# Moving the low-word bits and the squares of the values to ScalarE in an attention-and-experts kernel

## The chip, the cores and the metric

The kernel runs on one core of one Trainium2 chip, in one launch. The metric is the device time in microseconds; the median of three runs before the change is 773.28 us (770.98 to 773.47).

## The reference

The layer is causal attention with a gated memory, followed by two feed-forward layers:

```python
local = softmax(mask(q @ k.T / 8)) @ v                  # B, H, S, D = 2, 8, 576, 64
mem_out = (phi(q) @ M_prev) / (phi(q) @ z_prev + 1e-6)  # phi(x) = elu(x) + 1
x = g * mem_out + (1 - g) * local                       # g = sigmoid(beta), per head
x = relu(x @ moe_w_in) ** 2 @ moe_w_out                 # 1152 x 512 -> 2048 -> 512
out = sum_e p[:, e] * (relu(x @ w1[e]) @ w2[e])         # 4 experts, 512 -> 1024 -> 512
```

The values are float32, except `moe_w_in` and `moe_w_out`: they come as float64, so each of their numbers is a pair of 32-bit words in memory, and the kernel makes float32 of them on the chip.

## The kernel before

The 1152 tokens are nine tiles of 128, in three chunks: two tiles, then four, then three. Attention of a chunk runs beside the first feed-forward layer of the chunk before, so that TensorE always has something to do. Four stages follow each other: an opening with the attention of the first chunk, a stage in which the first feed-forward layer runs for that chunk (matmuls `hpa` and `y`) beside the attention of the second chunk, the same for the two later chunks, and then the experts.

The first of these feed-forward stages also converts the float64 weights (function `convert`). There are 16 blocks of 128 hidden units, each with an input half and an output half, so 32 halves. For each half SP issues the load of `w64` (128 x 512 pairs of words, 512 KB, four buffers). Line 626, on ScalarE, makes `mag`, the absolute value of the high word scaled by 2^-112. Line 628, on VectorE, makes `bits`, the low word shifted right by 29, which leaves its three upper bits. Line 629, on VectorE, shifts `mag` left by 3 and ors `bits` in; line 632, on VectorE, ors the sign in. Line 635 stores the half to `w1s` for the later chunks. Then `split` (lines 81 and 82) makes two parts of it for TensorE: line 81 on ScalarE, and line 82, the rest, on GpSimd for three quarters of the halves and on VectorE for the others.

`value_scale` (line 344 on) sums the squares of all values `v`, from which a power of two for scaling them is made. It takes ten tiles of 128 x 512, four of them through the two `vstage` buffers that SP fills; line 373 squares a tile on GpSimd into one of three `sq` buffers, line 363 adds it up on TensorE in the PSUM tile `total`, and line 380 on VectorE reduces it. `total` and the first `hpa` of the feed-forward layer share one PSUM buffer, so the first `hpa` can start only when line 380 is done.

What sets the order: TensorE's order is the program's own throughout. In the opening the order of all engines is written by hand as a string of steps, in which each `z` is one step of `value_scale`. Elsewhere a scheduler with its own costs orders VectorE, ScalarE, GpSimd and SP, and it also moves some later work up into the opening. Every engine runs its own list in order; an instruction that waits holds up all that stand behind it on that engine. The same holds for SP, where a load that waits for a free buffer holds up the loads behind it.

Other names: `sc` are the scores, `atp` their transposed form after exp, `pm` the memory product (line 330), `xm` its copy on ScalarE (line 333), `phia` phi of the queries (lines 163 to 166), `xy` the transposed output of attention, `r` and `g` the activated hidden units (lines 674 to 678).

Of the kernel before, what the change touches and what calls it, by code (L numbers as in the profile page):

```python
# [12 lines left out]
F16 = mybir.dt.float16  # L13
BF16 = mybir.dt.bfloat16
I32 = mybir.dt.int32
AF = mybir.ActivationFunctionType
ALU = mybir.AluOpType
AX = mybir.AxisListType
# [33 lines left out]
def attention_then_experts(ctx, tc, qa, ka, va, qc, kc, vc, mz, beta, w1, probs, w2, out):  # L52
# [11 lines left out]
    nc = tc.nc  # L64
# [15 lines left out]
    def split(w, raw, eng):  # L80
        nc.scalar.activation(out=w[:, 0], in_=raw, func=AF.Copy)  # L81
        eng.tensor_sub(w[:, 1], raw, w[:, 0].bitcast(F32))  # L82
# [25 lines left out]
    def power(s, r, z):  # L108

        nc.vector.tensor_single_scalar(out=s.bitcast(I32), in_=s.bitcast(I32), scalar=1, op=ALU.logical_shift_right)  # L110
        for x, op, zx in ((r, ALU.bitwise_and, 127 - z), (s, ALU.bitwise_xor, z)):
            nc.vector.tensor_scalar(
                out=x.bitcast(I32), in0=s.bitcast(I32), scalar1=0x7F800000, scalar2=0x3F800000, op0=ALU.bitwise_and, op1=op
            )
            nc.vector.tensor_scalar(out=x, in0=x, scalar1=2.0**-126, scalar2=0.5, op0=ALU.max, op1=ALU.min)
            nc.vector.tensor_scalar_mul(x, x, 2.0**zx)
# [35 lines left out]
    def gates():  # L152

        nc.scalar.activation(out=bt, in_=bt, func=AF.Exp, scale=-1.0)
        yield
# [5 lines left out]
    def phi(out, e, q):  # L161

        nc.scalar.activation(out=e, in_=q, func=AF.Exp)
        yield
# [10 lines left out]
    def combine(t, pool, xl, xm, sm, guard, pv, ps, eng, nm=1, gate1=gate1):  # L175
# [16 lines left out]
        def second():  # L192
# [4 lines left out]
            cs = slice(t * P, t * P + P)  # L197
            nc.scalar.activation(out=xy[:, 0, :, cs], in_=tp, func=AF.Copy)
            return lambda: nc.vector.tensor_sub(xy[:, 1, :, cs], tp, xy[:, 0, :, cs].bitcast(F32))
# [5 lines left out]
    def opening(c0, c1, first_layer):  # L205

        sc, ph, low, gt = [c0.scores(u) for u in c0.units], c0.phis(0), [], gates()
        later = [c1.scores(u) for u in c1.units[:4]]
        xs = []
        third = (slice(0, 3), slice(3, 6), slice(6, 8))  # L210
        steps = dict(
            g=lambda: next(gt), c=lambda: next(cv), w=lambda: next(first_layer), l=lambda: c1.load(1),
            x=lambda: xs.extend(c0.combine(c0.units[i][0]) for i in (0, 2)),
            a0=lambda: xs[0][0](), a1=lambda: xs[0][1](), a2=lambda: low.append(xs[0][2]()), a3=lambda: low[0](),
            b0=lambda: xs[1][0](), b1=lambda: xs[1][1](), b2=lambda: low.append(xs[1][2]()), b3=lambda: low[1](),
        )
        sv = []
        steps["z"] = lambda: next(sv[0]) if sv else (sv.append(value_scale(aap, c1.load_v)), next(sv[0]))
        for i in range(4):
            steps[f"s{i}"] = lambda i=i: next(sc[i])  # L220
            steps[f"t{i}"] = lambda i=i: c0.turn(c0.units[i], nc.vector)
            steps[f"v{i}"] = lambda i=i: c0.values(c0.units[i])
        for i in range(4):
            steps[f"S{i}"] = lambda i=i: next(later[i])
        for i in range(2):
            steps[f"p{i}"] = lambda i=i: next(ph[i])
        for i in range(3):
            steps[f"m{i}"] = lambda i=i: c0.mem(0, third[i])
        order = (
            "s0 p0 s1 g s0 g s2 s1 s0 s1 s2 s3 p1 s2 l s3 t0 z z p0 z x t1 S0 s3 t2 m0 p1 v0 z S0 t3 m1 "  # L230
            "m2 v1 z S1 z S2 z S0 v2 a0 b0 v3 z S3 S1 a1 z S1 b1 S2 a2 b2 z S3 c S3 S2 b3 w a3 z z c"
        )
        for k in order.split():
            steps[k]()

    def attention_a(c, pool, eng, banks):
# [28 lines left out]
        def s_(u):  # L265
# [22 lines left out]
            for i in range(nh):  # L288
                cs = slice(i * kn, i * kn + kn)
                nc.scalar.activation(  # L290
                    out=a[:, cs], in_=a[:, cs], func=AF.Exp, bias=nb[:, h0 + i:h0 + i + 1], scale=0.125,
                    accum_out=sm[:, h0 + i:h0 + i + 1],
# [3 lines left out]
        def t_(u, eng=None):  # L296
# [9 lines left out]
            else:  # L306
                nc.scalar.activation(out=at[:, 0:n], in_=tp[:, 0:n], func=AF.Copy)
            at_[u] = at
# [35 lines left out]
    def value_scale(pool, load_v):  # L344

        total = ps_h.tile([P, 512], F32, tag="h", name="total")
        ones = pool.tile([P, P], BF16, tag="ones", name="ones", bufs=1)
        nc.gpsimd.memset(ones, 1.0)
        parts = [va_t[b, r].rearrange("p h d -> p (h d)") for r in range(2) for b in range(B)]
        late = []  # L350

        def stage(b, k):
            x = pool.tile([P, 4, P], F32, tag="vstage", name="vstage", bufs=2)
            nc.sync.dma_start(out=x, in_=vc[b, :, :, k].rearrange("j p d -> p j d"))
            return x.rearrange("p j d -> p (j d)")

        todo = [(b, k) for k in (3, 4) for b in range(B)]
        n = len(parts) + len(todo) + B
        squares = []

        def add():
            i, sq = squares.pop(0)
            nc.tensor.matmul(total, lhsT=ones, rhs=sq, start=(i == 0), stop=(i == n - 1))

        for i in range(n):
            if 2 <= i < 2 + len(todo):
                parts.append(stage(*todo[i - 2]))
            if i == 4 + len(todo) - 2:
                load_v(2)
                parts += [va_t[b, 2].rearrange("p h d -> p (h d)") for b in range(B)]  # L370
            x = parts[i]
            sq = pool.tile([P, 512], BF16, tag="sq", name="sq", bufs=3)
            nc.gpsimd.tensor_mul(sq, x, x)
            if squares:
                add()
            squares.append((i, sq))
            yield
        add()
        yield
        nc.vector.tensor_reduce(out=vs, in_=total, axis=AX.X, op=ALU.add)  # L380
        power(vs, vi, 77)
        nc.vector.tensor_mul(gate1v, gate1, vi[:, 0:1].to_broadcast([P, H]))
        yield
# [224 lines left out]
    def convert(pool):  # L608

        todo = [x for g in range(n1 + 2) for x in ((g, 0), (g - 2, 1)) if 0 <= x[0] < n1]  # L610
        words = {}

        def fetch(i):
            if i < len(todo):
                f, half = todo[i]
                words[i] = pool.tile([P, DM, 2], I32, tag="w64", name="w64", bufs=4)
                nc.sync.dma_start(out=words[i].rearrange("p n t -> p (n t)"), in_=w1[f, half].bitcast(I32))

        for i in range(2):
            fetch(i)  # L620
        for i, (f, half) in enumerate(todo):
            fetch(i + 2)
            w64 = words.pop(i)
            mag = pool.tile([P, DM], F32, tag="mag", name="mag")

            nc.scalar.activation(out=mag, in_=w64[:, :, 1].bitcast(F32), func=AF.Abs, scale=2.0**-112)  # L626
            bits = pool.tile([P, DM], I32, tag="bits", name="bits", bufs=8)
            nc.vector.tensor_single_scalar(out=bits, in_=w64[:, :, 0], scalar=29, op=ALU.logical_shift_right)  # L628
            nc.vector.scalar_tensor_tensor(  # L629
                out=bits, in0=mag.bitcast(I32), scalar=3, in1=bits, op0=ALU.logical_shift_left, op1=ALU.bitwise_or  # L630
            )
            nc.vector.scalar_tensor_tensor(
                out=bits, in0=w64[:, :, 1], scalar=-(2**31), in1=bits, op0=ALU.bitwise_and, op1=ALU.bitwise_or
            )
            nc.sync.dma_start(out=w1s[f, half], in_=bits.bitcast(F32))
            made[f, half] = bits.bitcast(F32)
            yield
# [457 lines left out]
```

## Time and profile before

| | |
|---|---|
| median of three runs | 773.28 us |
| profiled execution, its own time | 768.09 us |
| its span | 766.3 us |
| busy: TensorE matmul | 706.8 us (92%) |
| busy: VectorE | 596.7 us (78%) |
| busy: ScalarE | 428.2 us (56%) |
| busy: GpSimd | 307.8 us (40%) |

The shares are means over stages with different limits. The experts fill the second half, where TensorE has almost no gaps. The conversion lies between 33 and 146 us, and in most of that stretch VectorE is busy all the time. In the page's slices of the span the TensorE clock is at its upper level, apart from the stretches behind a gap in TensorE's work.

### The profile page before, as it was taken

The page shows a single profiled execution, that of the slowest core. Times are in us where ns is not written, and L with a number is a line of the kernel's source. Part 1 is how long each engine was busy: PE and PEld are TensorE (multiplying, and loading weights), DVE is VectorE, ACT ScalarE, POOL GpSimd, SP SyncE. Part 2 cuts the span into 40 slices and gives each one's busy share as a digit, 9 for nine tenths or more (in the row PEclk, how much of TensorE's full clock was granted, in tenths as well). Part 3 has the DMA queues.
Part 4 walks back from the last instruction along what each step waited for, and adds up shares of the span by engine and source line. Part 5 has one row for each costly group of instructions (what it writes and reads, how often), then busy time and mean ns, then how long its engine had stood idle before and what let it go on. Part 6 is the DMA issues. An engine that isn't in the chain of part 4 may idle for free.

```text
span 766.3 us, 12975 instructions
## 1 busy us (share of the span) xinstructions
PE 706.8 (92%) x4740; PEld 511.8 (67%) x4740; DVE 596.7 (78%) x1114; ACT 428.2 (56%) x836; POOL 307.8 (40%) x303
## 2 busy tenths in 40 slices
PE   7679989897899999889989988989999999999997
PEld 5568878775677777888956555656665555555553
DVE  5869999769998875575786679999877777776763
ACT  4547666667656544786666565755544535344340
POOL 4445446444524147555532325443333132332300
PEclk9869899999999999999989999999999999999999
DMA  7666667266886563585421313323433223100002
GB/s 220 227 241 211 231 215 253 100 211 229 194 189 154 121 134 90 180 285 182 138 84 56 110 56 110 111 75 96 129 127 124 83 84 106 61 1 1 1 2 68
DMA packets 65425, 101.29 MB, mean 132 GB/s; under 512 B 32656, under 2 KB 34704, under 8 KB 65360
## 3 DMA queue, kind: packets, MB, share of 16 engines
q1 hardware_dynamic: 65216, 100.45, 42.9%
q8 instruction: 37, 0.61, 0.3%
q14 instruction: 28, 0.23, 0.1%
q10 hardware_dynamic: 144, 0.00, 0.0%
HBM read 82.87 MB, written 10.75 MB: 122 GB/s over the span
## 4 chain that ended last, share of the span: by engine, by line
PE 52%; DVE 25%; issue 7%; ACT 7%; POOL 4%; DMA 3%; SPq 1%; DVEq 0%; POOLq 0%; ACTq 0%
PE o L987 18%; PE pe L893 16%; PE y L685 6%; POOL w L82 2%; DVE a L171 2%; PE hpb L88 2%; DVE wu L857 2%; PE hpc L88 2%; PE hpa L88 2%; DVE bits L629 2%; PE pv L554 2%; DVE bits L628 1%; DMA raw<-in_w 1%; PE sc L277 1%; DVE h L914 1%
## 5 line engine op out<-in xcount | busy, mean ns | idle before, releaser
L987 PE MATMUL o<-w,g 128*128 128x512 f16 x864 | 220.2, 382 | 6.5 <-ACT junk L694 2.2
L893 PE MATMUL pe<-xs,wu 128*128 128x256 f16 (+1 forms) x1344 | 200.5, 289 | 5.8 <-DVE h L914 5.7
L893 PEld LDWEIGHTS <-wu 128*128 128x128 f16 x1344 | 132.6, 99 | 76.6 <-issue 9.8
L987 PEld LDWEIGHTS <-g 128*128 128x128 f16 x864 | 84.7, 99 | 77.0 <-issue 4.1
L685 PE MATMUL y<-g,w 128*128 128x256 f32 (+2 forms) x576 | 124.8, 350 | 1.3 <-POOL w L82 0.7
L82 POOL TENSOR_TENSOR w<-wraw,w 128x512 fp32r<-128x512 f32 x49 | 71.5, 1461 | 105.8 <-ACT w L81 98.0
L908 ACT ACTIVATE g<-h 128x512 f16<-128x512 f32 (+1 forms) x64 | 43.4, 678 | 109.2 <-DVE h L914 109.1
L685 PEld LDWEIGHTS y<-g,w 128*128 128x128 f32 x576 | 94.4, 191 | 11.8 <-POOL w L82 0.9
L923 POOL TENSOR_TENSOR u<-u,p 128x256 f32<-128x256 f32 (+1 forms) x32 | 30.3, 948 | 125.3 <-ACT p L922 114.9
L860 POOL TENSOR_TENSOR ws<-raw 128x256 f32<-128x256 f32 x32 | 24.7, 772 | 118.4 <-issue 97.8
L909 DVE SCALAR_TENSOR_TENSOR g<-h,g 128x512 f16<-128x512 f32 (+1 forms) x64 | 50.9, 796 | 22.1 <-ACT g L908 21.9
L914 DVE SCALAR_TENSOR_TENSOR h<-pe,u 128x256 f32<-128x256 f32 (+1 forms) x96 | 43.1, 452 | 24.3 <-PE pe L893 17.2
L88 PE MATMUL hpb<-xy,w 128*128 128x512 f32 x192 | 52.9, 411 | 7.1 <-DVE r L675 5.5
L857 DVE SCALAR_TENSOR_TENSOR wu<-ws,wpow,wu 128x512 f16<-128x512 f32 x64 | 50.5, 828 | 3.6 <-ACT wu L868 3.6
L793 DVE SCALAR_TENSOR_TENSOR w<-raw,wpow,w 128x512 f16<-128x512 f32 x64 | 48.2, 755 | 0.7 <-ACT w L792 0.6
L171 DVE CUSTOM_DVE_ANT_0 a<-sc,mask 128x384 f32<-128x384 f32 (+4 forms) x80 | 36.3, 476 | 15.7 <-PE sc L277 9.7
L82 POOL TENSOR_TENSOR w<-bits,w 128x512 fp32r<-128x512 f32 x24 | 37.7, 1570 | 26.2 <-ACT w L81 23.7
L88 PE MATMUL hpa<-xy,w 128*128 128x256 f32 x192 | 37.6, 323 | 10.9 <-ACT mag L626 7.1
L88 PEld LDWEIGHTS hpb<-xy,w 128*128 128x128 f32 x192 | 35.7, 194 | 16.8 <-DVE r L675 8.0
L792 ACT ACTIVATE w<-raw,wpow 128x512 f16<-128x512 f32 x64 | 45.1, 709 | 0.1
L81 ACT ACTIVATE w<-wraw 128x512 fp32r<-128x512 f32 x64 | 39.5, 623 | 9.9 <-PE y L685 7.4
L88 PE MATMUL hpc<-xy,w 128*128 128x384 f32 x192 | 39.3, 350 | 6.1 <-POOL w L82 2.5
(160 smaller groups left out, 1270.8 us busy)
## 6 DMA issues: line engine op xcount, KB each, us to landing
raw<-in_w SPq DMA_DIRECT2D x64, 512.0 KB, 3.4
w<-in_w SPq DMA_DIRECT2D x32, 512.0 KB, 4.3
wraw<-w1s SPq DMA_DIRECT2D x64, 256.0 KB, 3.0
w1s<-bits SPq DMA_DIRECT2D x32, 256.0 KB, 2.2
kraw<-in_kc SPq DMA_DIRECT2D x8, 576.0 KB, 4.2
vraw<-in_vc SPq DMA_DIRECT2D x8, 320.0 KB, 3.4
qraw<-in_qc SPq DMA_DIRECT2D x4, 512.0 KB, 4.1
out<-acc SPq DMA_DIRECT2D x8, 256.0 KB, 2.1
```

Of the source, the lines that this page charges most:

```text
L82: eng.tensor_sub(w[:, 1], raw, w[:, 0].bitcast(F32))
L88: nc.tensor.matmul(acc, lhsT=w[:, a, kk * P:(kk + 1) * P], rhs=xy[:, b, kk, t0:t0 + n], start=(i == 0), stop=(i == 3 * NK - 1),)
L171: nc.vector.tensor_tensor_reduce(out=dst, in0=sc, in1=msk, op0=ALU.add, op1=ALU.max, scale=1.0, scalar=-3.0e38, accum_out=m)
L685: nc.tensor.matmul(yacc[d], lhsT=w[:, a, d * P:(d + 1) * P], rhs=g[:, b], start=(f == 0 and i == 0 and d % per == 0), stop=(f == n1 - 1 an ...
L792: nc.scalar.activation(out=w0, in_=x, func=AF.Copy, scale=s)
L793: nc.vector.scalar_tensor_tensor(out=w1, in0=x, scalar=s, in1=w0, op0=ALU.mult, op1=ALU.subtract)
L857: nc.vector.scalar_tensor_tensor(out=w[:, 1, ks], in0=x, scalar=s1, in1=w[:, 0, ks], op0=ALU.mult, op1=ALU.subtract)
L893: nc.tensor.matmul(acc, lhsT=w[:, wa, k, kk * P:kk * P + P], rhs=x[:, xb, kk], start=(m == 0), stop=(m == 5))
L908: nc.scalar.activation(out=g[:, 0], in_=hm, func=AF.Relu)
L909: nc.vector.scalar_tensor_tensor(out=g[:, 1], in0=hm, scalar=0.0, in1=g[:, 0], op0=ALU.max, op1=ALU.subtract)
L914: nc.vector.scalar_tensor_tensor(out=out, in0=acc, scalar=HID, in1=x, op0=ALU.mult, op1=ALU.add)
L987: nc.tensor.matmul(outs[t], lhsT=g[:, gb, r:r + P], rhs=w[:, wa], start=(p == 0 and m == 1 and k == 0), stop=(p == 3 and m == 0 and k == 2),)
```

## The change

Two instructions move to ScalarE. Line 628 (line 630 after) becomes an activation with the function Copy: it reads byte 3 of the low word, which is its top byte, as an 8-bit integer at a stride of eight bytes, multiplies it by 1/32, subtracts 31/64 and writes the result as a 32-bit integer, which gives the same three bits. Line 373 (line 374 after) becomes an activation with the function Square. Buffers, loads and all matmuls stay.

```diff
-            nc.gpsimd.tensor_mul(sq, x, x)
+            nc.scalar.activation(out=sq, in_=x, func=AF.Square)
...
-            nc.vector.tensor_single_scalar(out=bits, in_=w64[:, :, 0], scalar=29, op=ALU.logical_shift_right)
+            nc.scalar.activation(out=bits, in_=w64.bitcast(U8)[:, :, 3], func=AF.Copy, scale=2.0**-5, bias=-31.0 / 64)
```

TensorE's list is the same instruction for instruction. On the other engines the scheduler's order changes up to the end of the conversion. Three places matter. (Line numbers after are one or two higher.)

ScalarE in the opening, from the exponentials of the second score tile on, before:

```order
L163 ACTIVATE phia<-qa 128x512
L290 ACTIVATE a,sm<-a,nb 128x128 x8
L333 ACTIVATE xm<-pm 128x3x2x65
L163 ACTIVATE phia<-qa 128x512
L333 ACTIVATE xm<-pm 128x3x2x65
L333 ACTIVATE xm<-pm 128x2x2x65
L290 ACTIVATE a,sm<-a,nb 128x256 x4
L198 ACTIVATE xy<-tp 128x4x128 x2
L626 ACTIVATE mag<-w_444 128x512
```

And from the same place after:

```order
L291 ACTIVATE a,sm<-a,nb 128x128 x4
L374 ACTIVATE sq<-va_0_153 128x512
L374 ACTIVATE sq<-va_0_155 128x512
L374 ACTIVATE sq<-va_1_232 128x512
L291 ACTIVATE a,sm<-a,nb 128x128 x4
L164 ACTIVATE phia<-qa 128x512
L334 ACTIVATE xm<-pm 128x3x2x65
L374 ACTIVATE sq<-va_1_234 128x512
L334 ACTIVATE xm<-pm 128x3x2x65
L334 ACTIVATE xm<-pm 128x2x2x65
L374 ACTIVATE sq<-vstage 128x512 x2
L164 ACTIVATE phia<-qa 128x512 x2
```

The squares now stand between the exponentials and behind the copies of `pm`; the squares of `vstage` come after the last of these copies.

SP in the opening, from the first two loads of `vstage` on, before:

```order
L354 DMA vstage<-in_vc 128x4x128 x2
L736 DMA mzt<-in_mz 64x1040
L354 DMA vstage<-in_vc 128x4x128
L250 DMA ka_705<-in_ka 128x512 x2
L354 DMA vstage<-in_vc 128x4x128
L259 DMA va_2_364<-in_va 128x512
L259 DMA va_2_366<-in_va 128x512
L617 DMA w_444<-in_w 128x1024
```

And after:

```order
L355 DMA vstage<-in_vc 128x4x128 x2
L738 DMA mzt<-in_mz 64x1040
L251 DMA ka_705<-in_ka 128x512 x2
L252 DMA qa<-in_qa 128x512 x2
L355 DMA vstage<-in_vc 128x4x128 x2
L260 DMA va_2_364<-in_va 128x512
L260 DMA va_2_366<-in_va 128x512
L618 DMA w_444<-in_w 128x1024
```

The later two loads of `vstage` stay ahead of the last values and of the first weights `w_444`; the loads of `ka` and `qa` moved up before them.

VectorE in the middle of the conversion, before (line 171 is the masked maximum over scores, line 286 its scaled negative for the exponential, line 675 the square of the hidden units):

```order
L632 SCALAR_TENSOR_TENSOR bits<-w_830,bits 128x512
L171 ISA a,mx<-sc,mask 128x384
L171 ISA mx 128x1
L675 SCALAR_TENSOR_TENSOR r<-hpa,r 128x256
L286 TENSOR_SCALAR nb<-mx 128x1
L628 TENSOR_SCALAR bits<-w_917 128x512
L82 TENSOR_TENSOR w_1034<-bits,w_1034 128x512
L629 SCALAR_TENSOR_TENSOR bits<-mag,bits 128x512
L171 ISA a,mx<-sc,mask 128x384
```

And after:

```order
L634 SCALAR_TENSOR_TENSOR bits<-w_830,bits 128x512
L677 SCALAR_TENSOR_TENSOR r<-hpa,r 128x256
L172 ISA a,mx<-sc,mask 128x384
L172 ISA mx 128x1
L287 TENSOR_SCALAR nb<-mx 128x1
L631 SCALAR_TENSOR_TENSOR bits<-mag,bits 128x512
L634 SCALAR_TENSOR_TENSOR bits<-w_917,bits 128x512
L83 TENSOR_TENSOR w_1034<-bits,w_1034 128x512
```

The shift is gone from VectorE's list; the two instructions that or the parts together now both come after ScalarE's two.

## Rows read from the trace of the kernel before

**Rows 1.** windows, busy us of each engine (instructions), granted clock, DMA
```profile
core 0: us, PE busy (x) PEld busy (x) DVE busy (x) ACT busy (x) POOL busy (x), PEclk, DMA share, GB/s
33.00:40.00 7.00, 0.09 (x1) 0.00 (x0) 6.76 (x16) 6.54 (x17) 1.81 (x2) 0.75 0.42 147
60.00:143.00 83.00, 75.05 (x681) 66.02 (x680) 81.23 (x164) 56.43 (x134) 43.73 (x34) 0.96 0.67 226
143.00:160.50 17.50, 17.04 (x167) 15.45 (x168) 10.46 (x27) 10.28 (x24) 7.08 (x7) 1.00 0.20 66
```

**Rows 2.** the chain that ended last, shares by line, in 100 to 120 us
```profile
by line: issue 24.7%; DVE bits L629 22.0%; DVE bits L628 18.6%; DVE a L171 12.0%; DVE bits L632 10.0%; DVE w L82 6.0%; DVE nb L286 3.2%; DVE xy L199 3.0%; ACT w L81 2.7%; ACT a L290 1.1%; DVE mx L171 0.5%; DVE r L675 0.4%; DVEq L628 0.2%; A
```

**Rows 3.** VectorE groups by form, 60 to 143 us: busy us, mean ns, idle
```profile
L628 DVE TENSOR_SCALAR bits<-w 128x512 int32<-128x512 int32 x24 | 20.2, 856 | 0.0
...
L629 DVE SCALAR_TENSOR_TENSOR bits<-mag,bits 128x512 int32<-128x512 int32 x24 | 20.5, 861 | 0.0
```

**Rows 4.** timeline of VectorE: start us, length us, instruction
```profile
118.18 0.41 DVE L628 TENSOR_SCALAR bits<-w 128x512 int32<-128x512 int32 x1
...
123.55 1.55 DVE L628 TENSOR_SCALAR bits<-w 128x512 int32<-128x512 int32 x1
```

**Rows 5.** timeline of GpSimd, the same place
```profile
123.53 1.28 POOL L82 TENSOR_TENSOR w<-bits,w 128x512 fp32r<-128x512 f32 x1
```

**Rows 6.** groups by form in 60 to 143 us, ScalarE
```profile
L626 ACT ACTIVATE mag<-w 128x512 f32<-128x512 f32 x24 | 15.9, 668 | 1.7 <-DMA w<-in_w 1.5 <-ACT at L307 0.2
```

**Rows 7.** timeline of ScalarE: two L626 one behind the other
```profile
131.85 1.26 ACT L626 ACTIVATE mag<-w 128x512 f32<-128x512 f32 x2
```

**Rows 8.** groups by form, whole run, ScalarE at 1024 elements
```profile
L868 ACT ACTIVATE wu<-ws,wpow 128x1024 f16<-128x1024 f32 x32 | 36.4, 1139 | 3.3 <-POOL ws L865 3.3
```

**Rows 9.** timeline of TensorE in the opening
```profile
13.60 1.06 PE L363 MATMUL total<-sq,ones 128*128 128x512 bf16 x2
14.46 1.09 PE L302 MATMUL atp<-ident,a 128*128 128x128 f32 x4
15.48 1.39 PE L277 MATMUL sc<-ka,qa 64*128 64x128 f32 x8
17.11 0.63 PE L302 MATMUL atp<-ident,a 128*128 128x128 f32 x4 [0.24 <-ACT a L290]
19.17 1.47 PE L330 MATMUL pm<-mzd,phia 128*128 128x130 f32 x6 [1.43 <-DVE phia L166]
...
22.86 1.28 PE L330 MATMUL pm<-mzd,phia 128*128 128x130 f32 x10
...
40.20 2.90 PE L88 MATMUL hpa<-xy,w 128*128 128x256 f32 x12 [7.11 <-ACT mag L626]
```

**Rows 10.** timeline of GpSimd in the opening
```profile
9.26 2.04 POOL L373 TENSOR_TENSOR sq<-va 128x512 bf16<-128x512 f32 x2 [4.91 <-DMA va<-in_va]
...
17.53 1.04 POOL L373 TENSOR_TENSOR sq<-vstage 128x512 bf16<-128x512 f32 x1 [0.19 <-PE atp L302]
```

**Rows 11.** timeline of ScalarE in the opening
```profile
16.98 0.39 ACT L290 ACTIVATE a<-a,nb 128x128 f32<-128x128 f32 x1
...
33.07 0.66 ACT L626 ACTIVATE mag<-w 128x512 f32<-128x512 f32 x1
```

**Rows 12.** timeline of the DMA queue (SP) in the opening: issues
```profile
18.60 0.38 SPq L354 DMA_DIRECT2D vstage<-in_vc  x1
...
24.85 1.39 SPq L617 DMA_DIRECT2D w<-in_w  x3
```

**Rows 13.** DMA issues in 0 to 60 us: count, KB each, us to landing
```profile
vstage<-in_vc SPq DMA_DIRECT2D x4, 256.0 KB, 4.7
```

**Rows 14.** the chain that ended last, in order of time, 38 to 53 us
```profile
39.45 0.60 DVE vs L380
...
46.75 4.37 POOL w L82
...
51.16 0.58 PE hpa L88
```

More of the change, by code (lines that the diff above doesn't have):

```diff
@@ L15 @@
 I32 = mybir.dt.int32
+U8 = mybir.dt.uint8
 AF = mybir.ActivationFunctionType
```

## The prediction

> **What bounds the kernel now.** I read the table of windows first, then the chain that ended last in the stretch that the change touches, then the groups and the order of time there, and at last the opening.
>
> The conversion divides the first 160 us into three. In 60 to 143 us VectorE is busy 81.2 of 83 us, TensorE 75.1, ScalarE 56.4, GpSimd 43.7 [rows 1]. TensorE's figure there is not its need: it passes 681 matmuls in 83 us, while behind the conversion, in 143 to 160.5, the same mixture goes through at 167 in 17.5 us with TensorE busy 17.04 of them [rows 1]. At that pace 681 take 681 x 0.105 = 71.4 us. So TensorE has some 11 us to spare, and VectorE, with 98% busy, is what the stretch lasts. The chain agrees: in 100 to 120 us it runs through VectorE, with L628 at 18.6% and L629 at 22.0% [rows 2]. From 143 on TensorE is the bound, and stays it for most of the rest; I expect nothing there but a shift.
>
> Before 60 us it is another matter: in 33 to 40 TensorE does next to nothing [rows 1], and its first `hpa` at 40.20 [rows 9] follows the end of the reduction of `total` at 39.45 + 0.60 on VectorE [rows 14], whose PSUM buffer it takes. (The row names a ScalarE instruction as releaser, but the `total` buffer fits to 0.15 us.)
>
> **The stretch of the conversion.** Removed there: 24 of the 32 shifts, 20.2 us of VectorE at a mean of 856 ns [rows 3]. One takes 0.41 us by itself, but 1.55 when it starts just behind a GpSimd instruction: the one at 123.55 lasts to 125.10, and GpSimd's, begun at 123.53, to 124.81 [rows 4, 5]. So of the 20.2 us about 24 x 0.41 = 9.8 are work and 10.4 are waiting for GpSimd. The work goes for certain. The waiting goes only if no other VectorE instruction meets the same GpSimd instruction in its place. L629 also lies at 861 ns [rows 3]. Bounds for what VectorE needs after: 81.2 - 20.2 = 61.0 us, and 81.2 - 9.8 = 71.4 us.
>
> The Trainium skill, "SBUF — State Buffer", section "Who interferes with whom", says that VectorE and GpSimd share one pair of ports, which an instruction holds to its end, and that VectorE wants it in its two-port modes and also for any two inputs from SBUF. The trace agrees as far as the pair at 123.5 us shows. By that rule L629 and L632, with two SBUF inputs each, inherit most of the waiting, and the upper bound is the better one; it would lengthen the stretch to no more than TensorE needs anyway.
>
> Added: 24 byte conversions on ScalarE. No row shows an 8-bit input. The nearest row is L626, which reads the same tile at the same stride of 8 bytes: 668 ns [rows 6], and two behind each other take 1.26 us, so 0.6 us each in a queue [rows 7]. As lower end I take 0.5, a little below the nearest row, since fewer bytes are read; as upper end 1.1, what an activation with twice the elements takes (1139 ns) [rows 8], for the case that small elements at a stride go at half the rate. I take 0.6, the nearest row. ScalarE's need becomes 56.4 + 24 x 0.6 = 70.8 us (68 to 83).
>
> So after the change three engines need about the same in this stretch: TensorE 71.4, ScalarE 70.8, VectorE 61 to 71. None can be beaten, so the floor is 71.4 and the most to be had 11.6 us. It will not come to the floor: VectorE reached 98% as the only full engine, but now VectorE's L629 waits for ScalarE, ScalarE's exponentials wait for VectorE's maxima, and both lists are in fixed order, so a wait of one passes to the other. I take 77 us (93% of the fullest): **-6 us**, ends 0 and -11.6.
>
> **The opening.** Removed: ten squares from GpSimd. Added: ten on ScalarE, at 0.6 us like the bytes. On GpSimd the first two ran at 9.26 for 2.04 us [rows 10], long before TensorE summed them at 13.60 [rows 9]. On ScalarE they stand behind the exponentials of the third score tile, so they start at 16.98, where now those of the fourth start [rows 11]. TensorE's list is unchanged: the two sums stand ahead of the transposes of 14.46, the scores and the transposes of 17.11. The second sum can start at 16.98 + 1.2 = 18.2 and ends at about 18.7; then 1.09 + 1.39 + 0.63 = 3.1 us of TensorE work follow, and the first `pm` starts at 21.8 instead of 19.17: 2.6 us late [rows 9]. It waited for VectorE's `phia` till 19.17, which the idle GpSimd would have let come earlier; that gain is covered by the sums.
>
> The second loss follows on SP. The first square of `vstage` ran at 17.53 [rows 10] and released the third `vstage` load at 18.60 [rows 12]. After, it stands behind the copies of all `pm`, whose last matmuls began at 22.86 and ran 1.28 [rows 9]: with the 2.6 late they end at 26.8, the copy at 27.3, and the square at 27.9. So the third load is issued at 27.9, 9.3 late; behind it in the queue are the fourth, the last values and the weights, whose issue goes from 24.85 [rows 12] to about 30. A `vstage` load lands 4.7 us after issue [rows 13], so the third arrives at 32.6. In ScalarE's list four squares, four exponentials and the two `xy` copies are still to follow before the first `mag`, ten at 0.6 us or a little less: 5.5 us. It goes from 33.07 [rows 11] to about 38, and with it the two halves, the reduction of `total` and the first `hpa`: 40.20 becomes about 45, **5 us late**.
>
> Part of this comes back at once. The third weight was late before: GpSimd's L82 began at 46.75 and took 4.37 us, and the third block's `hpa` had to wait for it to 51.16 [rows 14], 11.0 us behind the first. The two `phia` exponentials that stood between the conversions have moved up, and VectorE's part of `phia` with them, so GpSimd has less to fight with there and L82 can take the 1.28 us of rows 5, 3.1 less: 45 + 11.0 - 3.1 = 52.9 against 51.16. I take **+1.7 us** at 52.9 us; ends -1 (the loads land early) and +5 (nothing comes back).
>
> **Sum.** -6 + 1.7 = -4.3 us on the profiled execution's 768.09, of which the span is 766.3; that is 763.8. The median of the runs before is 773.28, higher by a factor 1.0068, and the same factor gives 769.0. I predict 769.0 us. A difference under 0.3% (2.3 us) can't be told from no change here.
>
> **The rivals.**
> - The waiting moves on. L629 and L632 take over the shift's waits, VectorE needs 71.4, ScalarE 70.8, and the waits between them cost more than I take: the stretch lasts 80, -3 + 1.7 gives 772.0. For it: L629 already lies 0.2 us above its unhindered time. Against it: GpSimd has as much time as before and fewer takers.
> - ScalarE becomes the bound at once. If the byte form takes 1.1 us, ScalarE needs 83 us, the stretch is what it was, and +1.7 remains: 775.0. Against it: an activation on 32-bit input at the same stride shows no such cost.
> - Slower: the opening isn't won back. It is the chain square, `vstage` load, weights: if the third load comes at 28 and the conversion starts with no lead, ScalarE has both to catch up and to serve the layer, so that every block's weights come just late; the stretch gains 1 us, the opening costs 5: +4, 777.3. It decides when the first `hpa` starts after 46 and the stretch still takes over 80. For it: ScalarE's need, 85% of the old stretch, leaves little to catch up with. Against it: the gap before 51.16 [rows 14] falls away whatever the lead.
> - TensorE at its floor: the stretch takes 72, -11 + 1.7: 763.9. For it: the scheduler has put exponentials and maxima early. Against it: three full engines in step.
> - That the change is none can be left out: the lists show the instructions moved.
>
> **Chances.** Forecast (765 to 771) 0.49, TensorE's floor 0.10, waiting moves on 0.13, ScalarE the bound 0.08, opening lost 0.20. Faster by over 0.3%: the first two less a small part of the forecast, 0.57. Within: the next two, 0.22. Slower: 0.21. The range takes in the floor's half and the slow case: 761 to 778; the forecast's own range is 765 to 771.5.
>
> **What the profile after would show.** The first `total` at 17.5 to 18 and the first `pm` near 21.8; the third `vstage` load issued near 28; the first `mag` near 38 and the first `hpa` near 45; the third block at 52 without the stall. The byte conversions at 0.65 us and 0.6 in a queue. In the stretch VectorE below 95%, ScalarE above 88%, L629 and L632 with a mean at or above 0.86, and the chain going through ScalarE and TensorE rather than VectorE alone. The first layer would end at about 156 instead of 160.5, and everything behind it keep its length. The prediction is wrong if the stretch keeps 83 us or falls under 73, or if `hpa` begins by 42 or only after 48.

## The result, and the profile after

The change makes the kernel faster, in one series by about what the forecast said and in the other by about twice as much. Median 759.69 us against 772.13 us of the kernel before in the same rounds (a quotient of 0.984); the ratio on record is 0.987, 95% interval 0.9824 to 0.9916. A second series (last experiment) gave 763.13 against 767.34, ratio 0.994, 0.9918 to 0.9962. By these ratios the gain is 0.6 to 1.3%, and the two intervals do not overlap, so series of one program differ by more than an interval says. 769.0 was forecast, 0.55% below the median that it started from (773.28), with a range of 761 to 778: 759.69 lies 1.3 us below that range, 763.13 in it. The profiled execution took 762.13 us (span 760.1), 6.0 less than the one before. (Line numbers after are one or two higher.)

Where the time went is read best from four marks in TensorE's order, which is the same in all these kernels: the starts of the first `hpa`, the first `hpb` (the first layer is over), the first `hpc`, and TensorE's last run of matmuls.

| start, us | first hpa | first hpb | first hpc | last run |
|---|---|---|---|---|
| before | 40.20 | 160.30 | 310.19 | 754.06 |
| after | 45.65 | 151.94 | 302.45 | 747.81 |
| difference | +5.45 | -8.36 | -7.74 | -6.25 |

So the opening lost 5.45 us, the first layer won 13.8, and 2.1 us were lost behind it, where the change touches nothing. (Each kernel's trace is one execution, and the first `hpa` varies from one to the next, as the last experiment shows.)

The windows of the kernel after come first, columns as in [rows 1]; the second ends where as many matmuls have passed as in 60 to 143 before:

```profile
33.00:40.00 7.00, 3.45 (x22) 2.19 (x20) 5.83 (x18) 6.73 (x20) 0.00 (x0) 1.00 0.71 276
...
60.00:133.50 73.50, 71.43 (x680) 63.20 (x679) 67.86 (x140) 65.00 (x153) 42.20 (x34) 1.00 0.74 249
...
134.00:152.00 18.00, 17.02 (x169) 15.31 (x168) 14.49 (x27) 12.60 (x30) 8.13 (x8) 1.00 0.26 83
```

The 680 matmuls that took 83 us [rows 1] now take 73.5. TensorE is busy 97% of that, VectorE 92%, ScalarE 88%. Of the 9.5 us, 5.9 are gaps of TensorE (7.95 before, 2.07 now) and 3.6 are its busy time (75.05 before, 71.43 now), the granted clock being 0.96 before and 1.00 now. The first 60 us end nearly level: 301 matmuls begun before, 298 after.

VectorE's and ScalarE's groups after, in 60 to 130 us, columns as in [rows 3]; the first fence is VectorE, the second ScalarE:

```profile
L634 DVE SCALAR_TENSOR_TENSOR bits<-w,bits 128x512 int32<-128x512 int32 x21 | 23.4, 1116 | 0.3
L631 DVE SCALAR_TENSOR_TENSOR bits<-mag,bits 128x512 int32<-128x512 int32 x20 | 20.5, 1026 | 3.8 <-ACT bits L630 3.6
```

```profile
L630 ACT ACTIVATE bits<-w 128x512 int32<-128x512 uint8 x21 | 14.1, 672 | 0.0
L627 ACT ACTIVATE mag<-w 128x512 f32<-128x512 f32 x21 | 14.1, 670 | 0.0
```

The byte conversion costs what the neighbour on 32-bit numbers costs. On VectorE the shift is gone, but the two instructions behind it have grown from 0.85 to 1.03 and 1.12 us: a half needed 0.81 + 0.85 + 0.86 = 2.52 us of VectorE before (means of the same window) and needs 2.14 after. Saved are 0.38 us, the shift's work without its waits. So the waits for GpSimd were handed on, as the Trainium skill's "SBUF — State Buffer", section "Who interferes with whom", lets expect of instructions with two inputs in SBUF.

The chain of waits after, shares by line, in 60 to 100 us and in 100 to 120 us:

```profile
by line: DVE bits L634 27.5%; issue 20.1%; DVE bits L631 17.2%; DVE a L172 10.9%; DVE r L677 4.6%; ACT bits L630 3.1%; DVE xl L190 3.0%; ACT mag L627 2.4%; DVE nb L287 2.3%; DVE w L83 1.7%; DVE xy L200 1.7%; ACT a L291 1.5%; ACT w L82 1.3%;
...
by line: PE sc L278 25.9%; PE y L687 25.3%; PE hpa L89 21.7%; PE pv L322 12.5%; PE atp L303 10.8%; DVE bits L634 2.6%; issue 2.2%; DVE mx L172 0.4%; DVE a L172 0.2%; DVEq L631 0.1%
```

VectorE still sets the first part; from 100 us on TensorE does, where before it was VectorE [rows 2].

The opening after, in order of time, first TensorE (the rows that answer to [rows 9]), then SP's issues (to [rows 12]):

```profile
18.27 1.10 PE L364 MATMUL total<-sq,ones 128*128 128x512 bf16 x2 [3.96 <-ACT sq L374]
...
20.16 2.07 PE L278 MATMUL sc<-ka,qa 64*128 64x128 f32 x8
22.17 1.12 PE L303 MATMUL atp<-ident,a 128*128 128x128 f32 x4
23.08 1.51 PE L331 MATMUL pm<-mzd,phia 128*128 128x130 f32 x6
...
45.65 2.90 PE L89 MATMUL hpa<-xy,w 128*128 128x256 f32 x12 [7.50 <-ACT mag L627]
...
53.25 0.62 PE L89 MATMUL hpa<-xy,w 128*128 128x256 f32 x3
```

```profile
29.17 0.93 SPq L355 DMA_DIRECT2D vstage<-in_vc  x2
...
31.16 1.38 SPq L618 DMA_DIRECT2D w<-in_w  x3
```

This is the forecast chain: late sums, late `pm`, late squares of `vstage`, late loads, late weights. What it cost came back before 60 us, because in the kernel before something else went wrong there. GpSimd before, at [rows 14]'s 46.75 (two L82 in one row), then VectorE before at the same place, and the windows before:

```profile
46.75 5.61 POOL L82 TENSOR_TENSOR w<-bits,w 128x512 fp32r<-128x512 f32 x2 [5.86 <-ACT w L81]
```

```profile
46.80 0.76 DVE L628 TENSOR_SCALAR bits<-w 128x512 int32<-128x512 int32 x2
47.47 1.29 DVE L629 SCALAR_TENSOR_TENSOR bits<-mag,bits 128x512 int32<-128x512 int32 x2
48.67 1.29 DVE L632 SCALAR_TENSOR_TENSOR bits<-w,bits 128x512 int32<-128x512 int32 x2
```

```profile
52.00:60.00 8.00, 8.00 (x57) 7.46 (x57) 3.53 (x10) 4.16 (x10) 3.03 (x4) 0.69 0.30 114
```

Six VectorE instructions ran back to back from 46.80 to 49.96, each at its unhindered time, and GpSimd's L82 did not get through until they were done. TensorE waited for it, and behind that gap its granted clock was 0.69 from 52 to 60. After, the same eight microseconds ran at full clock:

```profile
52.00:60.00 8.00, 7.61 (x81) 6.75 (x79) 7.93 (x11) 7.11 (x15) 4.09 (x4) 1.00 0.77 268
```

Behind the first layer 1.6 of the 2.1 us have a visible place, the first block of `hpc`, first before, then after:

```profile
310.91 3.22 PE L88 MATMUL hpc<-xy,w 128*128 128x384 f32 x17 [0.28 <-DVE xy L199]
```

```profile
303.18 4.78 PE L89 MATMUL hpc<-xy,w 128*128 128x384 f32 x17 [0.29 <-DVE xy L200]
```

The same 17 matmuls at two levels of the clock; in 302.45 to 308 the granted clock is 0.69. Of the 14 profiled executions of this study, 6 show 3.2 us here and 8 show 4.8, and the run with the byte conversion alone showed each once. So these 1.6 us belong to the execution and not to the change.

### The profile page after: what moved, and what is told of

It reads as the page before. It is cut to its first block, busy times and chain, and to the rows that moved or that the text cites. A ratio compares the mean times of both kernels' runs of the same rounds, so it can differ in the third digit from the quotient of the medians.

```text
span 760.1 us, 12986 instructions
## 1 busy us (share of the span) xinstructions
PE 706.0 (93%) x4740; PEld 511.6 (67%) x4740; DVE 584.4 (77%) x1082; ACT 448.6 (59%) x878; POOL 293.6 (39%) x293
## 4 chain that ended last, share of the span: by engine, by line
PE 55%; DVE 21%; ACT 9%; issue 7%; POOL 3%; DMA 3%; SPq 1%; DVEq 0%; POOLq 0%; ACTq 0%
PE o L989 18%; PE pe L895 16%; PE y L687 6%; PE hpb L89 3%; PE hpc L89 3%; DVE wu L859 2%; DVE bits L634 2%; PE pv L555 2%; DVE bits L631 2%; DVE a L172 2%; POOL w L83 1%; PE hpa L89 1%; PE sc L487 1%; PE sc L278 1%; DMA raw<-in_w 1%
## 5 line engine op out<-in xcount | busy, mean ns | idle before, releaser
L83 POOL TENSOR_TENSOR w<-wraw,w 128x512 fp32r<-128x512 f32 x49 | 72.2, 1475 | 107.2 <-ACT w L82 106.1
L89 PE MATMUL hpc<-xy,w 128*128 128x384 f32 x192 | 40.9, 361 | 6.1 <-POOL w L83 2.5
L82 ACT ACTIVATE w<-wraw 128x512 fp32r<-128x512 f32 x64 | 39.6, 624 | 11.0 <-PE y L687 8.8
L83 POOL TENSOR_TENSOR w<-bits,w 128x512 fp32r<-128x512 f32 x24 | 35.4, 1480 | 25.4 <-ACT w L82 25.4
L89 PE MATMUL hpa<-xy,w 128*128 128x256 f32 x192 | 35.7, 313 | 7.5 <-ACT mag L627 7.5
```

Of the source, the lines that this page charges most:

```text
L89: nc.tensor.matmul(acc, lhsT=w[:, a, kk * P:(kk + 1) * P], rhs=xy[:, b, kk, t0:t0 + n], start=(i == 0), stop=(i == 3 * NK - 1),)
```

## The experiments

My theory after the result: the layer won because VectorE's work went down to what TensorE needs, the waits only moved, and the squares on ScalarE gain nothing. (The or instructions below are the two that put the parts of a weight together, L629 and L632 before, L631 and L634 after.) The rivals: the squares do their share, or VectorE's waits for GpSimd still hold the layer, or ScalarE does.

### Each half of the change alone

`e1_bits_only`, the kernel after with the squares back on GpSimd:

```diff
-            nc.scalar.activation(out=sq, in_=x, func=AF.Square)
+            nc.gpsimd.tensor_mul(sq, x, x)
```

> The bits go to ScalarE, the squares stay on GpSimd. If the opening's delay is a loss that the first blocks only cover up, the first hpa starts at 39 to 41 us instead of 45.7, the layer from there to the first hpb lasts 107 to 110 us (120.1 before, 106.3 after), and the time is 3 to 5 us below the changed kernel. Rival: the third block's weights set the pace and the delay costs nothing, then the first hpa starts early but the first hpb comes at 152 all the same, and the time is that of the changed kernel within 2 us.

Measured: 757.06 us, ratio 0.981 (0.9765 to 0.9856). First `hpa` at 42.90, first `hpb` at 149.80: a layer of 106.9 us, as after the whole change (106.3), begun 2.75 us earlier. The byte conversion alone gives the gain of the layer. The first `hpa` came later than the 39 to 41 expected, and the time doesn't tell the two kernels apart: 2.6 us by the medians, with intervals that overlap, and each is 0.984 of the median before in its own rounds.

`e2_squares_only`, the kernel before with the squares on ScalarE (the same line the other way round).

> The squares go to ScalarE, the shift stays on VectorE. If the squares only delay the opening, the first hpa starts at 45 to 46 us, the layer lasts 115 to 120 us, and the time is 0 to 4 us above the kernel before. Rival: taking the squares off the port that GpSimd and VectorE share makes the opening faster, then the time is 1 to 3 us below before.

Measured: 765.66 us, ratio 0.994 (0.9913 to 0.9967): faster, so my expectation failed. The rival had the sign but not the reason, since the opening isn't faster: the first `hpa` starts at 42.25, 2 us late (I had expected 5 to 6), but the first `hpb` at 156.63, 3.7 us early. GpSimd, then VectorE, shows why, at the place of the stall:

```profile
47.20 1.36 POOL L82 TENSOR_TENSOR w<-bits,w 128x512 fp32r<-128x512 f32 x1 [4.28 <-ACT w L81]
...
49.40 1.75 POOL L82 TENSOR_TENSOR w<-bits,w 128x512 fp32r<-128x512 f32 x1
```

```profile
46.98 1.86 DVE L628 TENSOR_SCALAR bits<-w 128x512 int32<-128x512 int32 x2
```

L82 took 1.36 us. Here VectorE's two shifts, begun at 46.98, took 1.86 us instead of 0.76: one of them waited for GpSimd, not GpSimd for six of VectorE's. In 52 to 60 TensorE then had the full clock and 68 matmuls instead of 57:

```profile
52.00:60.00 8.00, 7.38 (x68) 6.63 (x67) 7.90 (x15) 4.83 (x11) 3.64 (x3) 1.00 0.81 266
```

So in these traces the squares won by moving the opening, so that one unlucky meeting came out the other way; the byte conversion breaks that meeting too, since the shifts are gone.

The layer comes apart at its fourth block. A block has 12 `hpa`; counted are the us from the first `hpa` to the 37th, and from there to the last, the 192nd, all by their starts:

| | first three blocks | fourth block to last `hpa` |
|---|---|---|
| before | 19.97 | 94.99 |
| e2_squares_only | 14.00 | 95.24 |
| e1_bits_only | 15.40 | 85.33 |
| after | 14.87 | 85.27 |

The squares alone win in the first three blocks, where the stall was, and nothing behind them; the byte conversion wins 9.7 us behind them, and spares the stall as well. (In a second execution of the last two kernels, `e11_bits_only_again` and `e12_change_again`, it was 15.40 and 15.38, 85.34 and 85.31.)

`e8_early_squares` is the kernel after with the first two `z` steps of the hand-written order, and the load step `l`, moved up to right behind the first tiles' exponentials:

```diff
-"s0 p0 s1 g s0 g s2 s1 s0 s1 s2 s3 p1 s2 l s3 t0 z z p0 z x ...
+"s0 p0 s1 g s0 g s2 l s1 s0 z z s1 s2 s3 p1 s2 s3 t0 p0 z x ...
```

> The changed kernel with the first two squares written earlier in the opening, behind the first tile's exponentials, where ScalarE waits for a load. TensorE's first two sums then come at 13 to 15 us instead of 18.3, the first pm at 19 to 22 instead of 23.1, the first hpa at 43 to 45 instead of 45.6. If the delay of the opening counts, the time falls by 1 to 2 us; if the first blocks take it up anyway (as the equal counts at 60 us say), it stays within 1 us of the changed kernel.

Measured: 757.36 us, ratio 0.9864 (0.9816 to 0.9912), which can't be told from the change's 0.987. The first `hpa` started at 42.75 instead of 45.65 and the first `hpb` at 149.08 instead of 151.94, so in its trace the 2.9 us were kept up to there; at the first `hpc` (301.88) only 0.6 of them are left, and the time of the rounds doesn't resolve it.

### How full are the engines

`e4_byte_twice`, the kernel after with the byte conversion done a second time into a tile that nothing reads:

```diff
+            twice = pool.tile([P, DM], I32, tag="twice", name="twice")
+            nc.scalar.activation(out=twice, in_=w64.bitcast(U8)[:, :, 3], func=AF.Copy, scale=2.0**-5, bias=-31.0 / 64)
```

> The changed kernel with each byte conversion done twice, the second into a tile that nobody reads: 32 x 0.55 to 0.6 us more on ScalarE, 14 us of it in the stretch. If ScalarE still has room there (its need 71 of 72 us says no), the layer lasts under 109 us; if ScalarE is as full as its sum says, the layer grows from 106.3 by 8 to 14 us and the time by as much.

Measured: 772.78 us, ratio 1.0029 (0.9989 to 1.0069), by the ratios 0.9 to 1.6% or 7 to 12 us over the changed kernel (its two series), and all of the gain gone. 32 conversions of 0.55 us in a queue are 17.6 us of ScalarE, of which 7 to 12 came out in the time. So I estimate that ScalarE had some 5 to 11 us to spare. The one trace (of an execution of 778.39 us) has the loss in the layer, which lasts 125.8 us:

```profile
60.00:130.00 70.00, 65.74 (x539) 58.45 (x540) 49.86 (x112) 59.89 (x137) 30.12 (x25) 0.84 0.60 199
```

But TensorE's granted clock was 0.84 there (1.00 after the change), and ScalarE was busy 59.89 us of 70, no more than after the change (61.91). How much of the loss is ScalarE's queue and how much the clock, this trace doesn't show, and no size is taken from it but the conversion's own, 0.67 us.

`e3_no_shift` is the kernel before with the shift taken from VectorE and given to nobody; the three low bits are missing from the weights (`zero` is a tile that is filled with zeros once, at the start):

```diff
-            nc.vector.tensor_single_scalar(out=bits, in_=w64[:, :, 0], scalar=29, op=ALU.logical_shift_right)
...
-                out=bits, in0=mag.bitcast(I32), scalar=3, in1=bits, op0=ALU.logical_shift_left, op1=ALU.bitwise_or
+                out=bits, in0=mag.bitcast(I32), scalar=3, in1=zero, op0=ALU.logical_shift_left, op1=ALU.bitwise_or
```

> The kernel before with the shift left out altogether: the instruction that ors the three bits in reads a constant tile of zeros in their place, so the low bits are missing in the weights; nothing is added to ScalarE. If VectorE's own work was what the shift cost and ScalarE has room for the bytes, the layer lasts 106 to 110 us as with the bits on ScalarE, and L629 and L632 rise from 0.86 us to 0.95 or more, since they inherit the waits for GpSimd. If ScalarE is the bound after the change, this one's layer is shorter than that by 3 us or more. If the waits vanish with the shift, L629 stays at 0.86 or below.

Measured: 757.54 us, ratio 0.9824 (0.9769 to 0.9879), no better than with the conversion on ScalarE. The two or instructions took 0.84 and 1.15 us (I had expected 0.95 or more of both), 0.28 us more than before in sum, so some of the shift's waits are among them. Its layer took 110.2 us, longer than the 106.3 after the change, and from the fourth block on 90.1 against 85.3; in 60 to 90 us its chain of waits holds 15.4% for loads of the weights, which the change's chain doesn't show. Had ScalarE been the bound after the change, this layer should have come out 3 us shorter or more; it is 3.9 longer, but the late loads hide what it would have been without them. Why the loads come late there I didn't follow up.

### What VectorE's waits are still worth

`e5_gpsimd_fills` leaves GpSimd its place in the first layer but makes its instruction one that only writes; the second parts of the weights are zero there:

```diff
-        eng.tensor_sub(w[:, 1], raw, w[:, 0].bitcast(F32))
+        if c == 0 and eng is nc.gpsimd:
+            nc.gpsimd.memset(w[:, 1].bitcast(F32), 0.0)
+        else:
+            eng.tensor_sub(w[:, 1], raw, w[:, 0].bitcast(F32))
```

`e6_no_sign` is the kernel after without the instruction that ors in the sign (L634; the signs of the weights are missing). `e7_before_gpsimd_fills` is the kernel before with the diff of `e5_gpsimd_fills`.

> The changed kernel, but in the first layer GpSimd fills its share of the weights' low parts with zeros instead of subtracting, so that it reads nothing there (the low parts of these weights are missing in the result). If VectorE's inherited waits for GpSimd bound the stretch after the change, L631 and L634 fall from 1.03 and 1.12 us to 0.7, VectorE's busy share in 60 to 130 us falls from 93% below 80%, and the layer from the first hpa to the first hpb shortens from 106.3 to under 103 us. If TensorE bounds it, the waits vanish just the same, but the layer keeps 105 to 107 us.

> The changed kernel without the instruction that ors the sign into the weights (the signs are missing): 32 x 0.6 us less on VectorE, ScalarE and GpSimd as they were. If VectorE bounds the stretch, the layer shortens from 106.3 by 3 to 8 us; if TensorE or ScalarE does, it stays within 2 us.

> The kernel before, with GpSimd filling zeros instead of subtracting as in the run above (low parts missing). It leaves the shift on VectorE and takes the waits away. If the shift cost the layer only its own 0.4 us each, the layer stays above 112 us (120.1 before). If the waits for GpSimd were as large a part, L628, L629 and L632 fall to 0.42, 0.69 and 0.69 us and the layer comes to 105 to 110 us, as far as moving the shift took it.

| | us | ratio (95%) | first hpa to first hpb | fourth block to last hpa |
|---|---|---|---|---|
| before | | | 120.1 | 94.99 |
| after | 759.69 | 0.987 (0.9824 to 0.9916) | 106.3 | 85.27 |
| e5_gpsimd_fills | 757.24 | 0.9848 (0.9803 to 0.9893) | 103.5 | 82.72 |
| e6_no_sign | 756.41 | 0.9841 (0.9804 to 0.9878) | 104.9 | 82.88 |
| e7_before_gpsimd_fills | 748.47 | 0.9744 (0.9698 to 0.979) | 101.6 | 82.89 |

The windows in 60 to 130 us carry the reading, first of the kernel after and of `e6_no_sign`, then, with VectorE's groups, of `e5_gpsimd_fills` (lines are three higher there) and of `e7_before_gpsimd_fills` (L631 is its shift):

```profile
60.00:130.00 70.00, 68.31 (x651) 60.60 (x650) 64.59 (x131) 61.91 (x145) 39.65 (x32) 1.00 0.75 249
60.00:130.00 70.00, 69.92 (x671) 62.04 (x670) 44.91 (x116) 64.12 (x150) 39.00 (x33) 1.00 0.79 259
```

```profile
60.00:130.00 70.00, 70.00 (x665) 62.41 (x665) 56.05 (x140) 64.58 (x153) 26.43 (x33) 1.00 0.78 260
...
L637 DVE SCALAR_TENSOR_TENSOR bits<-w,bits 128x512 int32<-128x512 int32 x22 | 18.8, 854 | 0.3
L634 DVE SCALAR_TENSOR_TENSOR bits<-mag,bits 128x512 int32<-128x512 int32 x22 | 16.0, 726 | 1.9 <-ACT bits L633 1.7
```

```profile
60.00:130.00 70.00, 69.86 (x671) 61.83 (x669) 64.40 (x156) 53.10 (x128) 23.16 (x31) 1.00 0.71 239
...
L632 DVE SCALAR_TENSOR_TENSOR bits<-mag,bits 128x512 int32<-128x512 int32 x22 | 15.7, 720 | 0.0
L635 DVE SCALAR_TENSOR_TENSOR bits<-w,bits 128x512 int32<-128x512 int32 x22 | 15.5, 714 | 0.0
L631 DVE TENSOR_SCALAR bits<-w 128x512 int32<-128x512 int32 x21 | 13.4, 650 | 0.3 <-DMA w<-in_w 0.3
```

With the waits or with an instruction taken from VectorE in the changed kernel, TensorE is busy 70.00 and 69.92 of 70 us, and the layer gets only 1.4 to 2.8 us shorter: after the change VectorE's waits cost 3 us at most. (The layer of `e5_gpsimd_fills` falls between the two cases that I had set, that of `e6_no_sign` in the case of TensorE or ScalarE as the bound.) In the kernel before they cost more: with the shift still on VectorE and most of the waits taken away, TensorE is full as well, and the layer is shorter than the 105 to 110 expected. From the fourth block on the three take the same 82.7 to 82.9 us, which I read as TensorE's floor; the change comes within 2.6 us of it, and `e7_before_gpsimd_fills` has the shorter layer because its first three blocks take 13.6 us and not 15.6 or 16.4. What bounded the layer before was the two engines getting in each other's way as much as the shift's own work: without most of the waits it is at the floor with the shift in place.

### Taking GpSimd out of the way without leaving work out

That points to a version to run: line 83 of the first layer all on VectorE. It adds work to VectorE but leaves GpSimd little to meet it with. The four were timed together on one chip, with the changed kernel and the byte conversion alone beside them:

```diff
-            on_vector = ((f % 4 == 3, f % 4 == 3), (f < 3, f % 4 == 3), (False, f % 2))[c][half]
+            on_vector = ((True, True), (f < 3, f % 4 == 3), (False, f % 2))[c][half]
```

> The changed kernel, but in the first feed-forward layer line 83 runs on VectorE for all halves instead of for a quarter of them, so that GpSimd no longer meets VectorE there except for g, xl and xm. If what is left of VectorE's waits is worth the 3 us that the runs with GpSimd memsets showed: L631 from 1026 and L634 from 1116 ns to about 0.72 us (41 x 0.35 = 14 us off in 60 to 130), 16 more L83 at 0.68 (11 us on), VectorE's busy time falls by some 3 us, TensorE is busy 69.5 or more of 70 us, the layer takes 103 to 105 us from first hpa to first hpb (106.3 after the change), and the time is 754 to 757, ratio 0.979 to 0.983. Rival: L83 waits for ScalarE's line 82 and in VectorE's list holds up the shift and the maxima behind it, so that the layer takes 107 or more, ratio 0.987 or above.

> The byte conversion on ScalarE, the squares on GpSimd as before the change, and line 83 of the first layer all on VectorE. If the squares on ScalarE are worth nothing beside the byte conversion, it is as fast as the run with the squares on ScalarE beside it, or up to 4 us faster because the first hpa starts at 42 to 43 instead of 45.6: 751 to 757, ratio 0.974 to 0.983. Rival: the squares on ScalarE win 0.6% here too, as they did alone, and this one is 3 to 5 us slower than the run beside it.

> The run with the byte conversion alone again, beside the changed kernel on one chip, to settle whether the squares take away part of its gain. If both edits fill the same ScalarE, the squares cost 1 to 4 us here: ratio 0.980 to 0.984 against 0.984 to 0.988 of the whole change. If the 0.6% that the squares won alone adds to it, this one is the slower of the two by 3 to 5 us.

> The changed kernel as it is, in the same series of rounds: ratio 0.984 to 0.988 by its first measurement (0.987, 0.9824 to 0.9916). If the byte conversion alone is better by 1 to 4 us it shows in this pair; if the squares add 0.6%, this one is 3 to 5 us faster than it.

| | squares on | line 83 on | us | ratio (95%) | first hpa | first hpb | first hpc | last run |
|---|---|---|---|---|---|---|---|---|
| e12_change_again | ScalarE | 3/4 GpSimd | 763.13 | 0.994 (0.9918 to 0.9962) | 44.61 | 151.46 | 304.46 | 749.35 |
| e11_bits_only_again | GpSimd | 3/4 GpSimd | 756.23 | 0.9847 (0.9826 to 0.9869) | 39.56 | 146.44 | 297.32 | 740.80 |
| e9_rest_on_vector | ScalarE | VectorE | 753.65 | 0.982 (0.9796 to 0.9844) | 43.06 | 146.02 | 295.95 | 741.45 |
| e10_bits_only_rest_on_vector | GpSimd | VectorE | 750.96 | 0.979 (0.9758 to 0.9822) | 42.33 | 146.52 | 295.72 | 737.35 |

The first two speak against the squares: beside the byte conversion they lose 6.9 us, with intervals apart, more than the 1 to 4 expected, and the changed kernel fell short of the 0.984 to 0.988 that I had expected of it. Not all of that is the squares' own price. Between the last two kernels it is 2.7 us, within their intervals. In the traces of the first two the layers are alike (106.9 each); of 8.6 us 5.0 are there at the first `hpa` and stay. ScalarE shows where: the first `mag` starts at 36.59 with the squares on ScalarE and at 31.52 without. But even there the squares have only a part: `e1_bits_only` and `e11_bits_only_again` are one program, and their first `hpa` lie 3.3 us apart, the first loads of `vstage` being issued at 11.36 and at 9.93. Over all traces with the byte conversion the first `hpa` starts at 43.06 to 45.65, mean 44.4, in the six with the squares on ScalarE in the change's order, and at 39.56 to 42.90, mean 41.6, in the three without: some 2.8 us. The rows, the changed kernel first:

```profile
36.59 0.65 ACT L627 ACTIVATE mag<-w 128x512 f32<-128x512 f32 x1
```

```profile
31.52 0.65 ACT L627 ACTIVATE mag<-w 128x512 f32<-128x512 f32 x1
```

The rest is the clock around the first `hpc`: 2.1 us in the 134 matmuls ahead of it, at a granted clock of 0.91 in `e12_change_again` and 1.00 in `e11_bits_only_again`, and 1.4 behind it. Windows and VectorE's groups of `e9_rest_on_vector` in 60 to 130 us:

```profile
60.00:130.00 70.00, 70.00 (x670) 62.00 (x669) 65.03 (x154) 64.42 (x149) 18.34 (x17) 1.00 0.75 252
...
L634 DVE SCALAR_TENSOR_TENSOR bits<-w,bits 128x512 int32<-128x512 int32 x22 | 17.6, 800 | 0.0
L83 DVE TENSOR_TENSOR w<-bits,w 128x512 fp32r<-128x512 f32 x21 | 17.2, 820 | 0.0
L631 DVE SCALAR_TENSOR_TENSOR bits<-mag,bits 128x512 int32<-128x512 int32 x21 | 14.3, 680 | 0.0
```

VectorE took on 16 more L83 and is no fuller than before that edit (65.03 against 64.6 us of 70); the or instructions fell from 1.03 and 1.12 us to 0.68 and 0.80. TensorE is at its floor (82.8 us from the fourth block on, 82.9 in the last of the four), and the layer lasts 103.0 us. The last of the four, with the squares on GpSimd, beats both kernels, 2.1% below the one before (1.8 to 2.4%); the step from `e9_rest_on_vector` to it is within their intervals.

## Why the prediction was right, and where it was small

The sign and the mechanism came as forecast; the size, 0.55%, is near that of the second series and under half of the first. In the profiled execution, where each term can be read:

- **VectorE is the bound of the stretch.** Right: every kernel that took work or waits from it, and gave ScalarE no more than one conversion a half, shortened the layer.
- **The work of the shift goes, its waits pass on.** Right. 0.38 us per half were saved, against the 0.41 forecast. That was the mechanism of the first rival, which priced it at 772.0; the price was wrong, since the rest of the waits weren't on the way any more.
- **The cost of the byte conversion.** Right: 0.67 us alone, 0.55 in a queue; the bound of 1.1 wasn't needed, and the rival that ScalarE becomes the bound at once falls. How near it was, `e4_byte_twice` only lets estimate.
- **The stretch takes 77 us (93% of the fullest engine).** Wrong, and this is the term that was mis-sized: it takes 73.5, 97% of TensorE's floor, so -9.5 instead of -6; four executions with the byte conversion agree to 0.1 us from the fourth block on. I had feared that three full engines in fixed order hand their waits to each other. They do little of that: `e5_gpsimd_fills` took most of VectorE's waits away and won 3 us. The rival of TensorE at its floor, with 72 us and a chance of 0.10, was nearer in the stretch than my forecast.
- **The opening: first `hpa` at about 45, third block at 52.9 against 51.16.** Right step by step: first `total` 18.27 (17.5 to 18), `pm` 23.08 (21.8; the scores ran 2.07 us instead of 1.39), third `vstage` load 29.17 (28), first `mag` 37.62 (38), first `hpa` 45.65. That it fits to 0.7 us is in part luck: two executions of one program start the first `hpa` 1.0 us apart (45.65, and 44.61 in `e12_change_again`) or 3.3 (`e1_bits_only`, `e11_bits_only_again`). What stood still until 51.16 before was the third `hpa` of the third block, which itself had begun at 47.03; the same matmul starts at 53.59 (52.9). The +1.7 carried to the end was too much: what I took for the end of the recovery was followed by a further one, since the kernel before ran on at a clock of 0.69 to 60 us. At 60 us the kernel after is 3 matmuls behind, 0.3 us.
- **The rest keeps its length.** Off by 2.1 us in the profiled execution, mostly the clock's level at the first `hpc`, which goes either way.
- **The signs.** The chain went through TensorE rather than VectorE only from 100 us on; in 60 to 100 us VectorE's L634 and L631 still hold 45% of it. The first layer ended at 151.94, not at 156.
- **What I didn't see.** That the two edits work against each other. I summed the gain of the stretch and the loss of the opening with one recovery between them, but either edit alone brings the recovery (no stall at 46.75). Against the kernel before, the later opening is hidden by it; against the byte conversion alone the squares are a loss, some 2.8 us at the first `hpa`. The third rival, the opening that isn't won back, is this mechanism; the slower time it gave didn't come, since ScalarE, at 88% in the stretch, kept up and the stretch took 73.5 us and not over 80.

In sum, -9.5 for the stretch, +0.3 up to 60 us, +0.8 in the matmuls between the stretch and the first `hpb` and +2.1 behind it make -6.3 in the profiled execution, where -4.3 was forecast. The sum is nearer than its terms: 3.5 us too little for the stretch and 2.1 us not foreseen behind it cancel in part.

## What to carry to other kernels

Where two engines hold each other up, count the time of both and ask what the freed time lets through: an instruction taken from the one shortens the list by its work, and its waits reappear on its neighbours until the other engine has less to do. Try the opposite move as well, taking the other engine's instructions onto the bound one, which here was worth 0.6 to 1.2% more (2.7 to 3.9 us of it in the layer itself). And time each edit of a joint change alone and on top of the other: one that gains by itself can lose beside another that cures the same stall.

## What the runs showed of the hardware that wasn't expected

- An 8-bit input at a stride of eight bytes costs ScalarE the same as a 32-bit one at that stride: 672 and 670 ns for 128 x 512.
- A GpSimd instruction that takes 1.3 us elsewhere took 4.37 us beside VectorE instructions that followed each other without a gap (six from 46.80 to 49.96 us), though it had begun 0.05 us ahead of them by the trace, while in `e2_squares_only`, at the same place in the program, VectorE's shift waited and GpSimd took 1.36 us. GpSimd's start differs by 0.45 us between the two; what decides who waits, the rows don't show.
- A GpSimd instruction that only writes (memset, 527 ns) hinders VectorE's or instructions less: they stood at 0.72 and 0.71 us beside it in `e7_before_gpsimd_fills` and at 0.73 and 0.85 in `e5_gpsimd_fills`, against 0.85 to 1.12 beside one with two inputs. The shift in `e7_before_gpsimd_fills` still took 0.65 us, where 0.41 is its time by itself.
- The same 17 matmuls behind the same 1.77 us gap ran in 3.22 to 3.24 us or in 4.78 to 4.80 us, one or the other in executions of the same program. What decides it stays open.
